# A long convolution and an MLP on one NeuronCore: the MLP in two passes through DRAM, its second layer with seven products for eight

## The chip, the cores and the metric

The kernel runs on one core of one Trainium2 chip. The metric is the device time of one execution in microseconds. Engines: TensorE (PE; its weight loads are PEld), VectorE (DVE), ScalarE (ACT), GpSimd (POOL) and SyncE (SP), which here issues almost all DMAs.

## The reference, cut to what matters

The first half (a layer norm, a short and a long causal convolution with gates) makes `x` of 2048 tokens and 640 columns. The second half, which the change touches, is a layer norm and an MLP with 1728 features:

```python
def _B_ref(x, w1, b1, w2, b2):
    h = jnp.einsum("bsd,df->bsf", x, w1) + b1
    zero = jnp.zeros_like(h)
    r = jnp.where(h > zero, h, zero)
    h = r * r
    out = jnp.einsum("bsf,fd->bsd", h, w2) + b2
    return out
...
h = _layernorm(x, axis=-1) * (1 + cb) + sb
x = x + gb * _B_ref(h, B_w1, B_b1, B_w2, B_b2)
```

## The kernel before, in words

Everything is float32. The first half works on five blocks of 128 columns; its order is written out in a table (`at`, with places `FS(b, j)` and `GS(b, s)`). It leaves the residual `x1` partly in SBUF and partly in the DRAM tile `x1_d`. The table's last places also load and split the first MLP weights.

The MLP multiplies in three terms: a number is split into a part in the type fp32r (`hi`, a copy by ACT) and the rest (`lo = x − hi`, a subtraction by DVE or POOL), and hi·hi, hi·lo and lo·hi are added up in PSUM. So each weight tile, each transposed input `XT` and each activation `h` costs one ACT copy and one subtraction.

The MLP runs over 8 chunks of 256 tokens (`NC`, `CH`) and, in each, over 14 groups of 128 features (`NF`; the last has 64). For one (chunk, group):

- `mlp_front` (L721): 5 blocks of input columns × 3 terms = 15 matmuls, stationary a 128x128 piece of w1, moving 256 tokens; the last group needs 10 (L712), the first two go through L735.
- `mlp_front_end` (L753, and L749 and L751 for the last group): ACT adds the bias and takes the positive part, out of PSUM; POOL squares it (`mul`, L150).
- `mlp_split` (L145, L156): ACT copy and DVE subtraction of 128x256.
- `mlp_back` (L791): three groups later (`MLAG`), stationary `h` of 128 features × 128 tokens, moving 320 columns of w2: 2 token halves × 2 column halves × 3 terms = 12 matmuls into four PSUM accumulators; the last group needs 8.

At a chunk's end `mlp_gate` (L806) multiplies the accumulators by the gate row, `mlp_out` adds the residual and stores. Beside the groups of one chunk run the statistics, the normalisation (`prep_hat`, L673), the transposes (`prep_xt1`, L686, L688) and the splits of the next one. The order is that of the loop at the end; `keep_order` fixes it on each engine, so an instruction that waits holds up all behind it on its engine. The helpers `copy` (L145), `mul` (L150), `add` (L153), `sub` (L156) and `sp_dma` (L138) record most operations. In the changed kernel the same helpers stand three lines lower.

Of the kernel before, what the change touches and what calls it, by code (L numbers as in the profile page):

```python
# [18 lines left out]
P = 128  # L19
# [4 lines left out]
NF = 14  # L24
# [3 lines left out]
MLAG = 3  # L28
# [64 lines left out]
def ssm_mlp_kernel(  # L93
# [38 lines left out]
    x1_d = dr.tile([S, D], F32, tag="x1_d", name="x1_d")  # L132

# [388 lines left out]

    ys, tss = {}, {}
# [62 lines left out]
    WI = {}  # L586
    slots = []

    def w_tile(tag, n):
        t = sb.tile([P, n * 1280], F32R, tag=tag, name=f"w_{tag}")  # L590
        for i in range(n):
            slots.append(t[:, 1280 * i : 1280 * (i + 1)])

    wn = [0, 0]
    stage = []

    def w_load(kind, f):
        m = P if f < NF - 1 else 64
        s = sb.tile([P, D], F32, tag="STG", name=f"w{kind}s_{f}", bufs=4)
        dst = slots.pop(0)  # L600
        if kind == 1:
            sp_dma(
                s[:, 0 : 5 * m].rearrange("p (k f) -> p k f", k=NB),
                w1[:, f * P : f * P + m].rearrange("(k p) f -> p k f", p=P),
            )
            s = s[:, 0 : 5 * m]
            d = dst[:, 0 : 10 * m].rearrange("p (h x) -> p h x", h=2)
            WI[1, f] = dst[:, 0 : 10 * m].rearrange("p (h k f) -> p h k f", h=2, k=NB)
            if m < P:
                s = s.rearrange("p (k f) -> p k f", k=NB)  # L610
                d = dst[:, 0 : 10 * m].rearrange("p (k h f) -> p h k f", h=2, k=NB)
                WI[1, f] = dst[:, 0 : 10 * m].rearrange("p (k x) -> p k x", k=NB)
        else:
            for j in range(P // m):
                sp_dma(s[j * m : (j + 1) * m], w2[f * P : f * P + m, :])
            d = WI[2, f] = dst.rearrange("p (h x) -> p h x", h=2)
        stage.append((kind, m, s, d))

    def w_high():
        kind, m, s, d = stage[wn[0]]  # L620
        wn[0] += 1
        copy(act, d[:, 0], s)

    def w_low(eng):
        kind, m, s, d = stage[wn[1]]
        stage[wn[1]] = None
        wn[1] += 1
        sub(eng, d[:, 1], s, d[:, 0])
        if kind == 2 and m == 64:
            dve.tensor_scalar(d[64:128, 1], s[64:128], 0.0, None, op0=ALU.mult)  # L630

    items = [(kind, f) for f in range(NF) for kind in (1, 2)]

    def load_item():
        if items:
            w_load(*items.pop(0))
# [25 lines left out]
    def load_x1(n):  # L662
        if n >= 2:
            X1t[n] = x1_tile(n)
            sp_dma(
                X1t[n], x1_d[n * CH : (n + 1) * CH, :].rearrange("(l p) d -> p l d", p=P)
            )

# [8 lines left out]
    def prep_xt(n, b):  # L677
        prep_xt1(n, b)
        prep_xt2(n, b)

    def prep_xt1(n, b):
        if b == 0:
            XT[n] = sb.tile([P, 2, NB, CH], F32R, tag=f"XP{(n + 1) % 2}", name=f"xt_{n}")
        t = ps.tile([P, 2, P], F32, tag="Y", name=f"xtp_{n}_{b}", bufs=2)
        for i in range(2):
            pe.transpose(t[:, i], ML["xh"][i][:, b * P : (b + 1) * P], ident)  # L686
        f = ML["xf"][b % 2]
        dve.tensor_scalar(  # L688
            f,
# [7 lines left out]
    def prep_xt2(n, b):  # L697
        f = ML["xf"][b % 2]
        copy(act, XT[n][:, 0, b], f)
        sub(pool, XT[n][:, 1, b], f, XT[n][:, 0, b])  # L700
# [3 lines left out]
    accs, hs, rs, hps = {}, {}, {}, {}  # L704

    def mlp_front(n, f, b):
        m = P if f < NF - 1 else 64
        if b == 0:
            hps[n, f] = ps.tile([P, CH], F32, tag="T", name=f"h_{n}_{f}", bufs=2)
# [63 lines left out]
    def mlp_back(n, f):  # L773
# [11 lines left out]
        if f == NF - 1:  # L785
            order.sort(key=lambda o: (o[0], o[2]))
# [481 lines left out]
```

## Time and profile before

| | |
|---|---|
| time, three runs | 701.93, 707.03, 709.17 us, median 707.03 |
| the profiled execution, its span from first to last instruction | 711.1 us |
| mean granted TensorE clock | 0.996 |
| instructions | 21018, of them 9164 matmuls |
| busy: PE, DVE, ACT, POOL | 660.6, 332.2, 330.2, 310.1 us |
| the part before the MLP's first matmul | 299 us |
| DMA | 74.75 MB, 105 GB/s in the mean |

Durations below come from the profiled execution. A row of a group gives line, engine, operation, the tiles it writes and reads with their shapes, the count, and its durations. The chain of waits is followed back from the last instruction; the releaser behind an idle time is what ended it.

### The profile page before, as it was taken

Reading aid. Unit: us, or ns where it says so; the run is one execution under the profiler, and the core shown is the slowest. Engines: PE = TensorE matmul, PEld = TensorE weight load, DVE = VectorE, ACT = ScalarE, POOL = GpSimd, SP = SyncE. Lnnn points to the kernel's source line nnn. Section 1 sums busy time; section 2 is a strip of 40 time slices with the busy share of each in tenths; the row PEclk is TensorE's granted clock in tenths of the full one; section 3 lists DMA queues with packets and bytes.
Section 4 is the critical chain, followed back from the end, with each engine's and each line's share of the span. In section 5 each row is a group of like instructions: output and inputs, shape, how many; then the busy total and the mean of one; then the engine's idle time right before and its main releaser. Section 6 shows DMA issues by size and latency. Waiting matters only on the chain.

```text
span 711.1 us, 21018 instructions
## 1 busy us (share of the span) xinstructions
PE 660.6 (93%) x9164; PEld 632.6 (89%) x9164; DVE 332.2 (47%) x601; ACT 330.2 (46%) x688; POOL 310.1 (44%) x390
## 2 busy tenths in 40 slices
PE   6698798998999988999999999999999999999997
PEld 5587697887889888889999999999999999999996
DVE  4275665657576677577532322322323332322313
ACT  4535556877876976357323333333233233233221
POOL 1071155469669858553522513414415315225213
PEclk9999999999999999999999999999999999999999
DMA  9797897689554644366020010010100200200101
GB/s 251 200 274 243 237 266 205 193 236 233 158 150 106 163 132 143 109 179 190 1 75 1 14 61 1 38 38 1 60 15 1 75 1 2 75 1 1 38 1 38
DMA packets 88720, 74.75 MB, mean 105 GB/s; under 512 B 19250, under 2 KB 73906, under 8 KB 88628
## 3 DMA queue, kind: packets, MB, share of 16 engines
q1 hardware_dynamic: 86672, 72.86, 35.7%
q8 instruction: 72, 1.18, 0.7%
q10 hardware_dynamic: 1892, 0.54, 0.3%
q14 instruction: 20, 0.16, 0.1%
q0 software_dynamic: 64, 0.01, 0.0%
HBM read 58.98 MB, written 14.42 MB: 103 GB/s over the span
## 4 chain that ended last, share of the span: by engine, by line
PE 86%; DVE 4%; ACT 4%; issue 3%; DMA 2%; POOL 0%; DVEq 0%; ACTq 0%; POOLq 0%; SPq 0%
PE acc L791 26%; PE h L721 25%; PE y L542 6%; PE pa L386 6%; PE x L401 5%; PE qp L467 5%; PE h L401 4%; PE t L531 3%; PE h L712 1%; PE xtp L686 1%; PE kt L242 1%; PE vt L279 1%; DVE wx L150 1%; DVE kacc L264 1%; PE gr L929 1%
## 5 line engine op out<-in xcount | busy, mean ns | idle before, releaser
L150 POOL TENSOR_TENSOR mtmp<-mtmp 128x256 f32<-128x256 f32 x112 | 71.5, 638 | 244.4 <-ACT mtmp L753 236.2
L721 PE MATMUL h<-xt,w_S 128*128 128x256 f32 x1290 | 167.6, 282 | 1.1 <-DVE w_S L156 1.1
L721 PEld LDWEIGHTS h<-xt,w_S 128*128 128x128 f32 x1290 | 161.7, 190 | 1.3 <-DVE w_S L156 1.3
L791 PE MATMUL acc<-w_S,hring 128*128 128x320 f32 x960 | 156.7, 311 | 0.2 <-DVE hring L156 0.2
L791 PEld LDWEIGHTS acc<-w_S,hring 128*128 128x128 f32 x960 | 142.1, 189 | 0.7 <-DVE hring L156 0.7
L156 DVE TENSOR_TENSOR hring<-mtmp,hring 128x256 fp32r<-128x256 f32 x112 | 66.4, 592 | 162.7 <-ACT hring L145 162.7
L753 ACT ACTIVATE mtmp<-h,b1t 128x256 f32<-128x256 f32 x104 | 49.3, 474 | 179.4 <-PE h L721 176.3
L145 ACT ACTIVATE hring<-mtmp 128x256 fp32r<-128x256 f32 x112 | 46.5, 416 | 48.8 <-POOL mtmp L150 47.8
L386 PE MATMUL pa<-wx,p 64*64 64x64 f32 x2560 | 51.0, 226 | 18.9 <-issue 11.8
L386 PEld LDWEIGHTS pa<-wx,p 64*64 64x64 f32 x2560 | 44.4, 138 | 26.1 <-issue 19.9
L145 ACT ACTIVATE a<-pa 128x512 f32<-128x512 f32 x80 | 43.3, 602 | 31.2 <-PE pa L386 30.7
L542 PE MATMUL y<-wx,wx 128*64 128x64 f32 x1280 | 45.2, 225 | 5.7 <-issue 4.4
L150 DVE TENSOR_TENSOR wx<-x,wx 128x512 f32<-128x512 f32 x64 | 41.0, 684 | 19.2 <-ACT wx L145 8.8
L542 PEld LDWEIGHTS y<-wx,wx 128*64 128x64 f32 x1280 | 40.4, 138 | 10.7 <-issue 6.7
L688 DVE TENSOR_SCALAR we<-xtp,cbs 128x256 f32<-128x256 f32 x35 | 19.0, 543 | 61.1 <-PE xtp L686 61.1
L401 PE MATMUL x<-a,gb 128*64 128x128 f32 x640 | 41.8, 274 | 2.9 <-DVE wx L150 1.8
L401 PEld LDWEIGHTS x<-a,gb 128*64 128x64 f32 x640 | 36.1, 137 | 4.1 <-PE h L401 2.4
L264 DVE SCALAR_TENSOR_TENSOR KV<-kt,tap,KV 128x511 f32<-128x511 f32 (+2 forms) x48 | 35.9, 748 | 8.0 <-ACT ktail L145 6.3
L145 ACT ACTIVATE q<-qp 128x512 f32<-128x512 f32 (+1 forms) x40 | 21.3, 584 | 33.4 <-PE qp L467 33.4
L156 POOL TENSOR_TENSOR we<-wx 128x256 f32<-128x256 f32 x20 | 15.8, 789 | 47.5 <-DVE wx L150 45.7
L153 POOL TENSOR_TENSOR wm<-wm,wm 128x640 f32<-128x640 f32 x20 | 32.6, 1631 | 8.7 <-ACT wm L344 8.4
L401 PE MATMUL h<-a,gb 128*64 128x128 f32 x512 | 34.9, 280 | 0.1
(142 smaller groups left out, 1026.3 us busy)
## 6 DMA issues: line engine op xcount, KB each, us to landing
wm<-in_w_mod_dram SPq DMA_DIRECT2D x25, 320.0 KB, 5.3
KV<-in_A_k_dram SPq DMA_DIRECT2D x20, 256.0 KB, 5.4
KV<-in_A_v_dram SPq DMA_DIRECT2D x20, 256.0 KB, 4.9
xp<-in_A_q_dram SPq DMA_DIRECT2D x5, 1024.0 KB, 7.5
out_dram<-x SPq DMA_DIRECT2D x14, 320.0 KB, 2.5
w1s<-in_B_w_dram SPq DMA_DIRECT2D x13, 320.0 KB, 3.7
w2s<-in_B_w_dram SPq DMA_DIRECT2D x13, 320.0 KB, 3.9
kv_d<-KV SPq DMA_DIRECT2D x16, 256.0 KB, 5.4
```

Source lines behind the costliest of these rows:

```text
L145: act.activation(o, i, AF.Copy)
L150: eng.tensor_mul(o, a, b)
L153: eng.tensor_add(o, a, b)
L156: eng.tensor_sub(o, a, b)
L264: dve.scalar_tensor_tensor(o, tk[:, : 512 - t], tap[:, b, t : t + 1], o, op0=ALU.mult, op1=ALU.add)
L386: pe.matmul(t[e][64 * r : 64 * r + 64, g].rearrange("p m d -> p (m d)"), pt[b][l, i, 8 * q + g, :], cw[l, r], start=True, stop=True,)
L401: pe.matmul(t[64 * a : 64 * a + 64, s + r], gb[:, g, r, a], AX[b][i][:, 2 * g + a], start=True, stop=True,)
L467: pe.matmul(t[a][:, u], gi[l, 4 * j + u, r], w[r][l, u % 2], start=(r == 0), stop=(r == 1),)
L542: pe.matmul(y[64 * h : 64 * h + 64, 4 * (g % 2) + i].rearrange("p c l d -> p (c l d)"), tss[g][:, i, 64 * r : 64 * r + 64], ca[:, r, h], s ...
L721: pe.matmul(hps[n, f][:m], WI[1, f][:, a, b], XT[n][:, x, b], start=(b == 0 and i == 0), stop=(b == NB - 1 and i == 2),)
L753: act.activation(r[:m], h[:m], AF.Relu, bias=b1t[:m, f : f + 1])
L791: pe.matmul(acc[2 * s + i], h[:, a, s * P : (s + 1) * P], w[:, y, i * 320 : (i + 1) * 320], start=(f == 0 and ti == 0), stop=(f == NF - 1 ...
```

## The change

**First pass.** Before anything of the second layer runs, the first layer is done for all tokens. A list `steps` gives its order: the first five feature groups for tokens 0 to 255 and 256 to 511 (ten steps of 256 tokens), the same groups for the other three tiles of 512 tokens (15 steps), then groups 5 to 8 and 9 to 13 for all four tiles (36 steps). A matmul moves 512 tokens from step 10 on. `mlp_front_end` squares on DVE up to step 24 and on POOL from then on, and stores the plain square to a DRAM tile `h_d`. The split of `h` is gone from this pass. All of `XT` stays in SBUF; w1 of the groups 9 to 12 goes into the slots of 0, 1, 2 and 5. The residual with `b2` times the gate is added per chunk (`resid`, one POOL operation of 1280 columns) and stored to `x1_d` again. Six chunks' residuals are fetched at the end of the first half.

**Second pass.** It goes over 8 chunks of 256 tokens and, in each, over six pairs of feature groups and one plain step for groups 12 and 13. A pair and two token halves and two column halves are a 2x2 block product, done with seven products of sums instead of eight. `w2_sums` forms the four sums on the w2 side once, in the first pass. `c_sums` forms four sums of 128x128 on the `h` side for each chunk and pair, on POOL, in a tile of seven such pieces; `c_split` makes hi and lo of all seven (128x896); `products` issues 7 × 3 matmuls into seven of eight PSUM accumulators, the plain step 20 into the last four. `evict_first` and `evict_rest` put the accumulators together. All eight PSUM banks are accumulators of one chunk. The loop runs ahead: `c_split` two steps, `c_sums` three, `c_load` four.

```diff
-MLAG = 3
+TW = 512
+NT = S // TW
+NP = 6
...
+    def c_sums(n, k):
+        if k == NP:
+            return
+        c = CT[n, k].rearrange("p (j s) -> p j s", j=7)
+        sub(pool, c[:, 4], c[:, 0], c[:, 1])
+        add(pool, c[:, 1], c[:, 1], c[:, 3])
+        sub(pool, c[:, 5], c[:, 1], c[:, 0])
+        sub(pool, c[:, 6], c[:, 2], c[:, 5])
+
+    def c_split(n, k):
+        c = CT.pop((n, k))
+        hi, lo = HT[n, k] = ML["h"][(7 * n + k) % 4]
+        if k < NP:
+            copy(act, hi, c)
+            sub(dve, lo, c, hi)
+            return
...
+        if k < NP:
+            for j, place in enumerate(PLACE):
+                c = slice(place * P, (place + 1) * P)
+                w = W2[k, j]
+                for i, (a, y) in enumerate(((0, 0), (0, 1), (1, 0))):
                     pe.matmul(
-                        acc[2 * s + i],
-                        h[:, a, s * P : (s + 1) * P],
-                        w[:, y, i * 320 : (i + 1) * 320],
-                        start=(f == 0 and ti == 0),
-                        stop=(f == NF - 1 and ti == len(terms) - 1),
+                        acc[j],
+                        h[a][:, c],
+                        w[:, y],
+                        start=(k == 0 and i == 0),
+                        stop=(k == NP - 1 and i == 2 and j < 4),
                     )
...
+    def evict_first(n):
+        acc = accs[n]
+        t1, t5, u2, u3, u4, v = (ML["e"][i] for i in range(6))
+        E[n] = t1, u3, u4, v
+        copy(act, t1, acc[0])
+        add(dve, u2, acc[1], t1)
+        copy(act, t5, acc[3])
+        add(dve, u3, acc[2], u2)
+        add(pool, u4, u2, t5)
+        add(pool, v, u3, t5)
...
+                add(dve, o[:, c], acc[4 + 2 * s + i], ((t1, u4), (u3, v))[s][i])
...
+                mul(dve, o, o, row0b)
+                add(pool, t[:, s], t[:, s], o)
+                sp_dma(out[(2 * n + s) * P : (2 * n + s + 1) * P, :], t[:, s])
...
+    def resid(n):
+        add(pool, X1t[n], X1t[n], row1b[0].unsqueeze(1).to_broadcast([P, 2, D]))
...
+    for m, (n, k) in enumerate(seq):
+        if m + 2 < len(seq):
+            c_split(*seq[m + 2])
+        if m + 3 < len(seq):
+            c_sums(*seq[m + 3])
+        if m + 4 < len(seq):
+            c_load(*seq[m + 4])
+        if k == 0:
+            x2_load(n)
+        products(n, k)
+        if k == NP - 1:
+            evict_first(n)
+        if k == NP:
+            evict_rest(n)
```

The order on POOL around the end of a chunk, before (`mtmp` is the ring of squares, `x1` the residual of a chunk, `gb2row` the gated bias row, `xt` the split input):

```order
L153 TENSOR_TENSOR x1_3_6008<-x1_3_6008,gb2row_4581 128x640
L150 TENSOR_TENSOR mtmp_4760<-mtmp_4760 64x256
L150 TENSOR_TENSOR mtmp_4760<-mtmp_4760 128x256 x2
L153 TENSOR_TENSOR x1_3_6008<-mtmp_4760,x1_3_6008 128x640
L150 TENSOR_TENSOR mtmp_4760<-mtmp_4760 128x256 x7
L156 TENSOR_TENSOR xt_5_7185<-we_69,xt_5_7185 128x256
```

and in the second pass of the change (`c_UP0` and `c_UP1` hold the pieces of two steps each, `e` the evicted accumulators, `wx1` the gated block, `wx2` the residual):

```order
L159 TENSOR_TENSOR c_UP1_5744<-c_UP1_5744 128x128
L156 TENSOR_TENSOR c_UP1_5744<-c_UP1_5744 128x128
L159 TENSOR_TENSOR c_UP1_5744<-c_UP1_5744 128x128 x2
L159 TENSOR_TENSOR c_UP0_5743<-c_UP0_5743 128x128
L156 TENSOR_TENSOR c_UP0_5743<-c_UP0_5743 128x128
L159 TENSOR_TENSOR c_UP0_5743<-c_UP0_5743 128x128 x2
L156 TENSOR_TENSOR e_2_6502<-e_1_6501,e_0_6500 128x320 x2
L159 TENSOR_TENSOR c_UP0_5743<-c_UP0_5743 128x128
L156 TENSOR_TENSOR c_UP0_5743<-c_UP0_5743 128x128
L159 TENSOR_TENSOR c_UP0_5743<-c_UP0_5743 128x128 x2
L156 TENSOR_TENSOR wx2_68<-wx2_68,wx1_67 128x640 x2
L159 TENSOR_TENSOR c_UP1_5744<-c_UP1_5744 128x128
```

One square per step has become four sums per step, and the eviction's four operations stand between the sums of the next chunk's steps 1, 2 and 3.

The order of SP's DMAs around the end of a chunk, before:

```order
L138 DMA out_0_dram<-x1_2_5507 128x640 x2
L138 DMA x1_4_6509<-x1_d_64 128x2x640
L138 DMA out_0_dram<-x1_3_6008 128x640 x2
L138 DMA x1_5_7010<-x1_d_64 128x2x640
L138 DMA out_0_dram<-x1_4_6509 128x640 x2
```

and in the second pass of the change:

```order
L141 DMA c_UP1_5744<-h_d_65 128x2x256
L141 DMA out_0_dram<-wx2_68 128x640 x2
L141 DMA c_UP1_5744<-h_d_65 128x2x256
L141 DMA wx3_69<-x1_d_64 128x2x640
L141 DMA c_UP0_5743<-h_d_65 128x2x256
L141 DMA c_UP0_5743<-h_d_65 128x256
L141 DMA c_UP0_5743<-h_d_65 64x256
```

Behind the two output stores now stands a load of `h` that the next chunk's step 4 needs; before, it was the next chunk's residual.

The order on POOL where the MLP starts, in the change (`xt` with a tag are the splits of the chunks 1, 2 and 3, `x1_2` and `x1_5` hold three chunks' residuals each, `xp_4` and `up_4` the first half's last block):

```order
L153 TENSOR_TENSOR gb2row_4575<-gb2row_4575,gbrow_4811 128x640
L156 TENSOR_TENSOR x1_0_2934<-x1_0_2934,gb2row_4575 128x1280
L156 TENSOR_TENSOR x1_1_2938<-x1_1_2938,gb2row_4575 128x1280
L159 TENSOR_TENSOR xt_S3_4536<-we_70,xt_S2_4510 128x256 x5
L156 TENSOR_TENSOR x1_2_4648<-x1_2_4648,gb2row_4575 128x1280
L159 TENSOR_TENSOR xt_KV_4927<-we_70,xt_KV_4927 128x256 x5
L156 TENSOR_TENSOR x1_2_4648<-xp_4_4037,up_4_4306 128x2x128
L159 TENSOR_TENSOR xt_KV_4927<-we_70,xt_KV_4927 128x256
L156 TENSOR_TENSOR x1_2_4648<-x1_2_4648,gb2row_4575 128x1280
L159 TENSOR_TENSOR xt_KV_4927<-we_70,xt_KV_4927 128x256 x4
```

Residual adds of 1280 columns now stand between the splits of the first chunks; before, POOL's squares of the first chunk and the last three adds of the first half stood here.

More of the change, by code (lines that the diff above doesn't have):

```diff
@@ L1144, in ssm_mlp_kernel @@
         )
-    for i in range(3):
-        w_tile(f"WX{i}", 1)
-    XT[0] = sb.tile([P, 2, NB, CH], F32R, tag="XP1", name="xt_0")
+    w_tile("WX0", 5)
     gate_sum(0, 3)
@@ L1151, in ssm_mlp_kernel @@
     tp += [tl[:, 0], tl[:, 1]]
[L1152 removed]
+    xf = ML["xf"] + [mt[:, 1280:1536]]
     def xt_f(b):
```

541 lines of the change are left out of this document (322 added, 219 removed).

## The prediction

> **What bounds the kernel now.** I read the page's first rows, then the stretches of the second half, then its chain and waits. In the stretch rows each engine has busy time and a count in brackets; then come TensorE's granted clock, the DMA share and GB/s.
>
> ```profile
> span 711.1 us, 21018 instructions
> PE 660.6 (93%) x9164; PEld 632.6 (89%) x9164; DVE 332.2 (47%) x601; ACT 330.2 (46%) x688; POOL 310.1 (44%) x390
> ...
> 298.95 3.99 PE L735 MATMUL h<-xt,w_S 128*128 128x256 f32 x30
> ...
> 303.00:317.50 14.50, 13.20 (x98) 12.50 (x96) 12.43 (x20) 9.16 (x19) 8.77 (x8) 1.00 0.59 169
> 450.30:501.40 51.10, 49.78 (x381) 49.55 (x381) 15.75 (x33) 16.61 (x37) 17.48 (x23) 1.00 0.07 27
> 705.20:711.10 5.90, 0.80 (x6) 0.53 (x4) 2.79 (x6) 0.00 (x0) 1.92 (x2) 0.85 0.30 111
> ```
>
> The MLP begins with its first matmul at 299.0 and lasts to 711.1: 412.1 us, the part that the change rebuilds. A chunk of 256 tokens takes 51.1 us, with PE busy for 49.8 at full clock, and POOL for only 17.5. PE is the bound.
>
> ```profile
> 317.51 1.76 PE acc L791 x12
> 319.27 1.76 PE h L721 x15
> 321.04 1.76 PE acc L791 x12
> ...
> 430.45 1.77 PE acc L791 x12
> 432.22 1.79 PE h L721 x15
> 434.23 1.76 PE acc L791 x12
> PE xtp L686 <- ACT mtmp L673: 7.9, 6, 1.3
> ```
>
> These are links of the chain (start, length). 15 matmuls of 256 columns take 321.04 − 319.27 = 1.77 us, 117.7 ns each; 12 of 320 columns take 1.76 us, 146.9 ns each. The difference is 0.456 ns a column, so the fixed part is 117.7 − 256 × 0.456 = 1 ns: time goes by columns, not by matmuls. Two transposes put in cost 434.23 − 432.22 − 1.79 = 0.22 us.
>
> The 412.1 us are thus: first layer 8 chunks × (13 × 15 + 10) = 1640 matmuls, 193.0; second layer 8 × (13 × 12 + 8) = 1312, 192.7; 35 pairs of transposes, 7.7; tail 5.9; and 12.8 in which PE stands still, 7.9 of it before transposes.
>
> **The change part by part.** *First layer.* A matmul takes 512 columns where it took 256, so 1640 become 150 of 256 and 745 of 512. By the slope a wide one costs 2 × 117.7 = 235.4 ns and nothing is gained. Bounds: no fixed part at all, or one of at most 31 ns, the period of the smallest matmuls of this trace (64 in 2.0 us):
>
> ```profile
> 8.79 2.00 PE pa L386 x64
> ```
>
> That would be worth 745 × 31 ns = 23 us. I take zero, by the two rows whose matmuls are of the same kind. The Trainium skill ("TensorE: Matmul & The Clock Gate", section on the back-to-back issue gap) gives columns/2.4 + 2.5 ns, so 215.8 for 512; by it pass one would be 745 × 19.6 ns = 14.6 us shorter, but it also gives 135.8 for 320 columns where this trace has 146.9.
>
> *Second layer.* Per chunk, 6 pairs of feature groups × 7 products × 3 terms = 126 matmuls, and 20 for the last two groups: 146 for 164. Over 8 chunks 1168 × 146.9 ns = 171.6 us, 21.1 less. This is the whole gain that PE can show; it is PE work on the path, so it counts in full if operands arrive. A chunk's PE time becomes 21.45 us.
>
> *What feeds it.* Each of the 48 steps (21 matmuls, 3.08 us of PE) now needs four POOL sums of 128x128, a ScalarE copy of 128x896 and a VectorE subtraction of 128x896. ScalarE first:
>
> ```profile
> L145 ACT ACTIVATE hring<-mtmp x112: 399/418/421, 304.1 to 703.4; 128x256 fp32r<-128x256 f32 x104, 64x256 fp32r<-64x256 f32 x8
> L145 ACT ACTIVATE w_S<-w1s x11: 720/730/740, 248.5 to 328.5; 128x640 fp32r<-128x640 f32 x11
> ```
>
> 0.42 at 256 and 0.73 at 640 give 0.94 at 896, hidden under 3.08 of PE. POOL (min/median/max in ns):
>
> ```profile
> L153 POOL TENSOR_TENSOR p<-p,dsm x8: 208/235/721, 8.5 to 220.9; 128x8 f32<-128x8 f32 x4, 128x32 f32<-128x32 f32 x4
> L156 POOL TENSOR_TENSOR xt<-we,xt x35: 733/739/1187, 330.3 to 651.0; 128x256 fp32r<-128x256 f32 x35
> L153 POOL TENSOR_TENSOR wm<-wm,wm x20: 1534/1550/2002, 101.7 to 242.4; 128x640 f32<-128x640 f32 x20
> L153 POOL TENSOR_TENSOR x<-mtmp,x x9: 857/1572/1582, 354.8 to 706.6; 128x640 f32<-128x640 f32 x7, 128x320 f32<-128x320 f32 x2
> 39.67 0.73 POOL L156 TENSOR_TENSOR we<-wx 128x256 f32<-128x256 f32 x1
> 40.36 0.72 POOL L153 TENSOR_TENSOR we<-wx 128x256 f32<-128x256 f32 x1
> 148.22 3.17 POOL L153 TENSOR_TENSOR wm<-wm,wm 128x640 f32<-128x640 f32 x2 [4.91 <-ACT wm L344]
> ```
>
> 8, 256, 320 and 640 columns take 0.21, 0.73, 0.86 and 1.55: 0.2 plus 2.1 ns a column, so 0.46 at 128. The trace has no 128; the bounds are 0.36 (half of 256) and 0.73 (256 itself), and the line through four rows decides for 0.46. Independent neighbours start 0.69 apart for 0.73 of work; two that depend take 3.17 for 2 × 1.55, 0.05 extra. Three of the four sums wait for the one before: 0.46 + 3 × 0.51 = 1.99 us a step. A chunk's eviction adds two 320-wide sums and two 640-wide adds: 2 × 0.86 + 2 × 1.55 = 4.8. POOL alone: 6 × 1.99 + 4.8 = 16.8 us, below 21.45.
>
> But VectorE and POOL collide:
>
> ```profile
> 304.05 1.29 POOL L153 TENSOR_TENSOR xp<-xp,up 128x512 f32<-128x512 f32 x1
> 304.57 1.05 DVE L156 TENSOR_TENSOR hring<-mtmp,hring 128x256 fp32r<-128x256 f32 x1 [4.49 <-ACT hring L145]
> 305.29 0.80 POOL L150 TENSOR_TENSOR mtmp<-mtmp 128x256 f32<-128x256 f32 x1
> 305.56 1.21 DVE L156 TENSOR_TENSOR w_S<-w1s,w_S 128x640 fp32r<-128x640 f32 x1
> 306.06 1.87 POOL L153 TENSOR_TENSOR xp<-xp,up 128x512 f32<-128x512 f32 x1
> L156 DVE TENSOR_TENSOR hring<-mtmp,hring x112: 412/426/1679, 304.6 to 703.9; 128x256 fp32r<-128x256 f32 x104, 64x256 fp32r<-64x256 f32 x8
> L150 POOL TENSOR_TENSOR mtmp<-mtmp x112: 606/613/1191, 303.5 to 702.8; 128x256 f32<-128x256 f32 x104, 64x256 f32<-64x256 f32 x8
> L806 DVE TENSOR_TENSOR mtmp<-acc,gbrow x32: 477/482/492, 353.8 to 706.9; 128x320 f32<-128x320 f32 x32
> ```
>
> The subtraction that takes 0.43 alone ends at 305.62, 0.28 after the POOL add that ends at 305.34; POOL's next ends at 306.09, 0.47 after it; the 640-wide at 306.77, 0.68 after that. They take turns, whole instruction by whole instruction. The multiply that reads one operand from PSUM never slows (477 to 492). The Trainium skill ("SBUF — State Buffer", the section on SBUF's two sides) has this rule: the port pair that the two engines share is an exclusive lock held for the whole instruction, by a VectorE operation with two SBUF inputs as well. The rows agree; without that lock the chunk's POOL time would stay 16.8.
>
> Held time is 0.28 at 256 and 0.68 at 640, so 0.95 at 896; POOL's next sum then starts prepared (0.47 for the square that alone takes 0.61, 0.13 back), and the 0.05 of dependence is hidden: 0.77 a step. With the two 640-wide multiplies by the gate (0.68 − 0.13 each) and two 256-wide subtractions (0.15 each), 6 × 0.77 + 1.4 = 6.0 a chunk. POOL with its waits: 22.8 us against PE's 21.45. So POOL falls behind by up to 1.4 us a chunk.
>
> *At a chunk's end* POOL stands in order behind two adds that need the finished block; queued behind them are the sums for step 3 of the next chunk. SyncE stands behind the output stores, and queued there is the load for step 4:
>
> ```profile
> x_d<-xp SPq DMA_DIRECT2D x15, 256.0 KB, 3.4
> KV<-in_A_k_dram SPq DMA_DIRECT2D x20, 256.0 KB, 5.4
> ```
>
> From the block's last matmul: a VectorE sum (0.48) and two 640-wide multiplies (0.43 + 0.40 each) 2.1, POOL adds 3.1, issue 0.4, load 3.4, sums 2.0, copy and subtraction 0.94 + 1.09, together 13.0 us, against four steps of PE, 12.3: 0.7 late, 2.7 with the slower load. With the 1.4 that POOL falls behind I take 2.0 a boundary, 14 for seven, between 0 (POOL's backlog absorbed in its lead of three steps, loads in time) and 19 (the slow load each time).
>
> *Start and entry.* In the first 15 steps POOL must do the row product (1.6), six residual adds of 1280 columns (2.9 each), 25 splits (0.70), three adds (0.73), and give way to VectorE for ten 256-wide squares (0.15), five 512-wide (0.42) and two weight splits (0.55): 43.4 us, from here on:
>
> ```profile
> 299.93 1.58 POOL L150 TENSOR_TENSOR gb2row<-gb2row,gbrow 128x640 f32<-128x640 f32 x1 [7.87 <-ACT gbrow L145]
> 305.00:320.00 15.00, 13.70 (x101) 13.06 (x100) 12.99 (x22) 9.29 (x19) 7.86 (x8) 1.00 0.73 212
> ```
>
>  PE needs the last split at 299.0 + 3.5 + 8 × 1.77 + 5 × 3.53 + 25 × 0.22 + 2.8 = 342.6. POOL is through at 343.3 if it never waits, and it will wait for the copies ahead of its splits: 1 to 8 us of stall, I take 4. Traffic there is 3 MB of fetched residual, stores and weights, near the 212 GB/s that the second row has, which could cost a few us of the 8.
>
> In the rest of pass one a step's work is hidden under 3.53 of PE: POOL's square of 512 (1.2), at times two weight sums of 320 (0.86 each) beside it. h is 1728 × 2048 × 4 bytes = 14.2 MB, out and back some 70 GB/s over 400 us, where the steady row above has 27 and the start's 212: hidden too, except for the load at the boundary. On entering pass two POOL has the squares of the last two steps among its first sums: those for step 2 end some 6 us in, copy and subtraction make it 8, and PE is there at 6.2: about 2. The tail gets one more 320-wide addition, 0.5.
>
> *Sum.* 193.0 + 7.7 + 171.6 + 6.4 + 4 + 14 + 2 = 398.7, for 412.1: 13.4 less. The profiled span, 711.1, lies 4.1 above the median shown, 707.0; I take the same saving off that: 693.6, rounded to 693.5.
>
> **Rivals.** (1) *POOL keeps up*: PE never waits at boundaries, and start and entry cost 6 together. 384.7, a saving of 27.4: 679.6 us. For it: POOL alone needs 16.8 of 21.45. Against it: the alternation above.
> (2) *Wide matmuls are cheaper*: a fixed part near 20 ns, 15 us beyond the forecast: 678.5. Against it: the two-row slope.
> (3) *What TensorE saves is given back*: sums of 0.55 instead of 0.46 put POOL at 24 × 0.09 = 2.2 more, 25.0 us a chunk, 3.5 beyond PE: 25 for seven where I have 14, and a start of 6 for 4: 693.5 + 11 + 2 = 706.5, no change. For it: 0.55 lies inside the bounds. Against it: the line.
> (4) *POOL sets the pace, slower*: if a 128-wide sum costs nearly what a 256-wide one does, a step is 0.73 + 3 × 0.78 + 0.77 = 3.84 and a chunk 23.0 + 6.2 = 29.2, 7.8 beyond PE; seven are 55 where I have 14: 734. It decides from 0.58 a sum on: (0.58 − 0.46) × 24 = 2.9 more a chunk, 20 in seven, which against the saving of 13.4 puts the time 7 above now. For it: VectorE is one more claimant in that queue, and every sum waits on semaphores. Against it: the four rows on one line.
>
> **How the numbers follow.** The forecast gets 0.47 with its own range 684 to 703, rival 1 0.15, rival 2 0.05, rival 3 0.15, rival 4 0.18. A measurement here tells about 1% from no change, so faster means under 700 and slower above 714. Most of the forecast, with rivals 1 and 2, is faster: 0.60. Rival 3 and the forecast's edge: 0.21. Slower: 0.19. Below 678 lies a tenth; above 722 another, rival 4's upper half: the range is 678 to 722.
>
> **What would show it.** In the changed profile: 512-column matmuls 235 ns apart (216 would be rival 2); 128-wide POOL sums of 0.46 alone and chains of four near 2.0, stretched to 2.8 when the 896-wide subtraction falls among them; that subtraction at 1.1 alone and up to 1.5 when it waits; chunks of pass two 23 to 24 us long with PE busy for 21.5; PE's waits in pass two on VectorE's and ScalarE's split, steps 3 and 4 of a chunk first; POOL busy for over 85% there. A pass two with chunks of 21.5 means rival 1, of 25 or more rivals 3 or 4. A stall at one place above 8 us, or pass one over 215 us (I have 205), would make the prediction wrong.

## The result and the profile after

| | before | after |
|---|---|---|
| median of 4 runs, us | 706.7 (701.9 to 709.2) | 747.2 (745.1 to 752.3) |
| ratio | | 1.057, 95% interval 1.051 to 1.063 |
| profiled execution: span, time | 711.1 | 744.6, 746.3 |
| first matmul of the MLP | 298.95 | 296.07 |
| from there to the first product of pass two | | 235.0 |
| from the first product to the end of the span | | 213.5 |

The change makes the kernel 5.7% slower, 40.5 us by the medians. I had forecast 693.5 us, and a range up to 722.

The first rows of the page after the change, to be read beside those of before:

```profile
span 744.6 us, 19800 instructions
PE 658.9 (88%) x8275; PEld 588.3 (79%) x8275; DVE 408.9 (55%) x634; ACT 335.0 (45%) x631; POOL 440.9 (59%) x545
```

TensorE has 889 matmuls fewer in the records, most of those of the first layer twice as wide, and is busy for about as long (658.9 for 660.6). POOL went from 310 to 441 us, VectorE from 332 to 409.

The stretches of the MLP on one table (busy time and count for each engine, granted TensorE clock, DMA share, GB/s):

```profile
303.00:315.00 12.00, 6.32 (x48) 5.59 (x47) 8.92 (x17) 3.99 (x11) 5.84 (x6) 0.97 0.40 151
315.00:328.00 13.00, 10.41 (x53) 10.12 (x54) 9.98 (x18) 5.39 (x12) 6.68 (x7) 0.64 0.14 50
328.00:340.00 12.00, 7.92 (x46) 7.04 (x45) 6.89 (x16) 6.04 (x12) 8.74 (x9) 0.86 0.16 57
340.00:355.00 15.00, 11.89 (x52) 9.28 (x51) 7.20 (x16) 6.60 (x13) 8.25 (x7) 0.89 0.42 138
367.00:384.00 17.00, 12.06 (x51) 9.16 (x50) 11.23 (x19) 8.52 (x15) 7.96 (x7) 0.90 0.39 119
400.00:522.00 122.00, 122.00 (x538) 100.58 (x537) 35.95 (x50) 43.67 (x83) 57.85 (x57) 1.00 0.38 120
582.50:608.40 25.90, 23.80 (x148) 22.87 (x148) 14.07 (x17) 6.98 (x10) 20.49 (x29) 0.93 0.38 120
738.30:744.60 6.30, 0.01 (x1) 0.00 (x0) 3.30 (x7) 0.00 (x0) 0.86 (x1) 0.70 0.30 105
```

Three things stand here. From 400 to 522 us pass one runs without a stall, as forecast: TensorE is busy for 122.00 of 122.00, at full clock. Before that, in the steps in which the transposes of the later chunks are made, it stands still for a fifth to a half of a stretch and its clock sinks, at the lowest to 0.64. And a chunk of pass two lasts 25.9 us for the 21.45 of matmuls that I had counted. Its clock of 0.93 is not the reason: three of the chunks have 0.93 or 0.94 and last 25.9 to 26.4 us, three have 1.00 and last 25.8 to 26.0.

What TensorE waits for from 296 to 389 us (us, times, longest), and the links of the chain in that time (start, length):

```profile
PE xtp L725 <- DVE we L726: 19.5, 7, 4.9
PE h L775 <- ACT xt_S L148: 2.9, 1, 2.9
PE xtp L725 <- ACT mtmp L718: 1.4, 3, 0.5
```

```profile
303.85 2.88 DVE wx L153
...
317.01 2.82 DVE wx L153
...
369.05 2.99 DVE wx L153
...
388.86 133.31 PE h L775 x585
```

The long stall is at the transposes, which wait until VectorE has emptied their two PSUM tiles (L726). VectorE comes late because of squares (`wx`, L153) that last 2.8 to 3.0 us. The timeline of one such place shows why:

```profile
303.53 2.92 POOL L156 TENSOR_TENSOR x<-x,gb2row 128x1280 f32<-128x1280 f32 x1 [1.86 <-ACT mtmp L718]
303.85 2.88 DVE L153 TENSOR_TENSOR wx<-wx 128x256 f32<-128x256 f32 x1 [1.49 <-ACT wx L806]
306.65 0.41 DVE L156 TENSOR_TENSOR x<-xp,up 128x256 f32<-128x256 f32 x1
306.99 1.61 DVE L726 TENSOR_SCALAR we<-xtp,cbs 128x256 f32<-128x256 f32 x3
307.58 0.44 PE L725 MATMUL xtp<-ident,mtmp 128*128 128x128 f32 x2 [2.10 <-DVE we L726]
```

POOL adds the bias row to a chunk's residual in one operation of 1280 columns, 303.53 to 306.45. A square of 256 columns that VectorE starts at 303.85 ends at 306.73, just after POOL has done. The evictions stand behind it in VectorE's order, the transposes behind those in TensorE's order, and with them every matmul. At the longest wait, 4.9 us until 375.31, the square holds VectorE from 369.05 to 372.04, and 2.7 us of a later chunk's statistics still stand between it and the evictions.

At a chunk's end, the links of the chain (after the last matmul) and SyncE's queue with what POOL does meanwhile (the first view leaves out links under about a microsecond):

```profile
582.88 1.67 DVE wx L156 x4
584.55 1.04 DVE wx L153
586.47 1.23 issue
587.71 2.42 POOL wx L156
590.59 3.71 DMA c_UP<-h_d
597.97 1.20 POOL c_UP L156
601.25 1.10 DVE h_XP L159
602.40 3.06 PE acc L864 x19
```

```profile
585.66 4.46 POOL L156 TENSOR_TENSOR wx<-wx,wx 128x640 f32<-128x640 f32 x2 [0.76 <-DVE wx L153]
586.24 2.46 DVE L159 TENSOR_TENSOR h_x<-c_UP,h_x 128x896 fp32r<-128x896 f32 x1
587.77 2.72 SPq L141 DMA_DIRECT2D out_dram<-wx  x2
590.59 0.65 SPq L141 DMA_DIRECT2D c_UP<-h_d  x1
```

The forecast had this chain; but POOL's two additions take 4.46 us, not 3.1, while an 896-wide subtraction of VectorE falls among them and lasts 2.46 for 1.09: the two take turns.

### The profile page after: what moved, and what is told of

Its sections match the earlier page's. It is cut to its first block, busy times and chain, and to the rows that moved or that the text cites. A ratio compares the mean times of both kernels' runs of the same rounds, so it can differ in the third digit from the quotient of the medians.

```text
span 744.6 us, 19800 instructions
## 1 busy us (share of the span) xinstructions
PE 658.9 (88%) x8275; PEld 588.3 (79%) x8275; DVE 408.9 (55%) x634; ACT 335.0 (45%) x631; POOL 440.9 (59%) x545
## 4 chain that ended last, share of the span: by engine, by line
PE 54%; DVE 13%; DMA 10%; ACT 7%; POOL 7%; issue 6%; SPq 1%; DVEq 0%; POOLq 0%; ACTq 0%
PE h L775 21%; PE pa L389 5%; DMA c_UP<-h_d 5%; PE acc L864 5%; PE qp L470 4%; DVE wx L153 4%; PE y L566 4%; PE x L404 4%; POOL wx L156 3%; PE acc L877 3%; PE h L404 3%; POOL c_UP L159 2%; PE t L555 2%; DVE wx L156 2%; DVE s L302 2%
## 5 line engine op out<-in xcount | busy, mean ns | idle before, releaser
L159 POOL TENSOR_TENSOR c_UP<-c_UP 128x128 f32<-128x128 f32 x144 | 91.3, 638 | 36.2 <-DMA c_UP<-h_d 26.6
L153 POOL TENSOR_TENSOR wx<-wx 128x512 f32<-128x512 f32 (+1 forms) x36 | 40.5, 1124 | 73.5 <-ACT wx L806 68.4
L775 PE MATMUL h<-xt_S,w_S 128*128 128x512 f32 (+1 forms) x285 | 77.7, 378 | 3.1 <-ACT xt_S L148 2.9
L806 ACT ACTIVATE wx<-h,b1t 128x512 f32<-128x512 f32 (+1 forms) x57 | 36.8, 647 | 85.0 <-PE h L775 78.0
L864 PE MATMUL acc<-w_S,h_S 128*128 128x320 f32 x360 | 60.2, 318 | 9.6 <-ACT h_S L148 5.7
L389 PE MATMUL pa<-wx,p 64*64 64x64 f32 x2560 | 52.7, 233 | 14.1 <-issue 8.3
L864 PEld LDWEIGHTS acc<-w_S,h_S 128*128 128x128 f32 x360 | 54.7, 192 | 13.3 <-ACT h_S L148 7.0
L159 DVE TENSOR_TENSOR h_S<-c_UP,h_S 128x896 fp32r<-128x896 f32 (+2 forms) x32 | 37.3, 1170 | 49.6 <-ACT h_S L148 49.5
L775 PEld LDWEIGHTS h<-xt_S,w_S 128*128 128x128 f32 x285 | 51.4, 211 | 10.0 <-ACT xt_S L148 3.1
L148 ACT ACTIVATE a<-pa 128x512 f32<-128x512 f32 x80 | 43.3, 601 | 29.5 <-PE pa L389 29.4
L153 DVE TENSOR_TENSOR wx<-x,wx 128x512 f32<-128x512 f32 x64 | 41.0, 684 | 16.9 <-ACT wx L148 6.5
L566 PEld LDWEIGHTS y<-wx,wx 128*64 128x64 f32 x1280 | 40.4, 138 | 10.7 <-issue 6.5
L153 DVE TENSOR_TENSOR wx<-wx 128x512 f32<-128x512 f32 (+1 forms) x25 | 28.6, 1149 | 34.5 <-ACT wx L806 34.5
L775 PE MATMUL h<-xt_XP,w_S 128*128 128x512 f32 x120 | 41.2, 394 | 0.0
L864 PE MATMUL acc<-w_S,h_x 128*128 128x320 f32 x180 | 31.8, 327 | 9.0 <-ACT h_x L148 5.9
```

The lines of the kernel that those rows point to most:

```text
L148: act.activation(o, i, AF.Copy)
L153: eng.tensor_mul(o, a, b)
L159: eng.tensor_sub(o, a, b)
L389: pe.matmul(t[e][64 * r : 64 * r + 64, g].rearrange("p m d -> p (m d)"), pt[b][l, i, 8 * q + g, :], cw[l, r], start=True, stop=True,)
L566: pe.matmul(y[64 * h : 64 * h + 64, 4 * (g % 2) + i].rearrange("p c l d -> p (c l d)"), tss[g][:, i, 64 * r : 64 * r + 64], ca[:, r, h], s ...
L775: pe.matmul(hps[key], w, y, start=(b == 0 and i == 0), stop=(b == NB - 1 and i == len(terms) - 1),)
```

## The experiments

Each row below is one profiled execution (the last kernel's time is a median of 6). "First stretch" goes from the MLP's first matmul to the first product of pass two, "chunk" is the mean of seven chunks of pass two, "rest" goes from the first product to the end of the span. The first column shows how far the work before the MLP, which none of the edits touches, moves from execution to execution: 291.1 to 301.2 us. That is why causes are read from the stretches and not from the whole; the forecast for the whole was missed more than once (s3, b1, w1) where that for the stretch or the chunk was met or nearly met. Kernels that share a part show how far it moves by itself: the unchanged first stretch 235.0 to 236.4 (after, b1, b2, b4), the repaired one 209.3 and 210.0 (d1, d2), the unchanged rest 212.5 to 215.2 (after, s1, s2, s3, d1), the repaired one 184.1 to 184.3 (b4, d2, w1).

| kernel | MLP begins | first stretch | chunk | rest | time |
|---|---|---|---|---|---|
| after | 296.1 | 235.0 | 25.8 | 213.5 | 746.3 |
| s1 no residual addition | 298.7 | 220.9 | 26.0 | 215.2 | 736.7 |
| s2 residual in pieces | 291.3 | 226.1 | 25.6 | 212.5 | 731.5 |
| s3 squares by ScalarE | 291.1 | 217.3 | 25.8 | 213.2 | 723.4 |
| b1 late stores | 293.7 | 236.2 | 23.7 | 198.8 | 730.5 |
| b2 additions by VectorE | 301.2 | 235.9 | 24.4 | 203.4 | 742.7 |
| b4 both of these | 294.7 | 236.4 | 21.6 | 184.3 | 717.6 |
| d1 start repaired | 296.7 | 209.3 | 25.8 | 213.5 | 721.3 |
| d2 all repairs | 293.0 | 210.0 | 21.6 | 184.1 | 688.9 |
| w1 d2, 256-wide matmuls | 300.1 | 216.7 | 21.6 | 184.3 | 702.9 |
| f1 d2, last squares moved | 294.5 | 208.1 | 21.6 | 182.6 | 687.0 |

The chunk's mean comes from the first and the last of the 16 copies by which ScalarE empties two accumulators a chunk. The last is the second copy of its chunk and comes nine matmuls of 146.9 ns, 1.3 us, after the first one. In the kernel after the change, (734.1 − 552.2 − 1.3) / 7 = 25.8:

```profile
L148 ACT ACTIVATE e<-acc x16: 417/428/438, 552.2 to 734.1; 128x320 f32<-128x320 f32 x16
```

### The start: who holds the port

The theory: POOL's addition of 1280 columns holds the port that the two engines share, and VectorE, working in order, carries the wait on to the transposes. The rivals: latency of the chain or traffic (A), the amount of POOL's work whatever its pieces (B), VectorE's statistics and ScalarE's rows (C).

**s1.** The addition is left out, so the output lacks that term.

```diff
     def resid(n):
-        add(pool, X1t[n], X1t[n], row1b[0].unsqueeze(1).to_broadcast([P, 2, D]))
+        return
```

> Left out: the addition of the gated bias row to the residual (eight POOL additions of 128x1280, 2.95 us each, between 296 and 389 us), so the output lacks that term. Theory (these additions hold the port that POOL and VectorE share; VectorE's squares and statistics stand behind them, its evictions of the transposes stand behind those, and TensorE waits): the stall of 33 us in the first 93 us of the MLP shrinks by 20 or more, pass one lasts 205 to 212 us instead of 232, the whole 718 to 727 us. Rival A (the stall is the delay of a chain of small hand-overs, or traffic of the residual): at most 6 us less, pass one 226 or more, the whole above 738. Pass two: chunks of 26 us as before by either.

The first stretch fell by 14.1 us, to 220.9: more than rival A allows, less than I had expected. VectorE's groups from 296 to 389 us, first in the kernel after the change, then (298 to 392) in this one:

```profile
L153 DVE TENSOR_TENSOR wx<-wx 128x512 f32<-128x512 f32 x8 | 12.0, 1499 | 11.4 <-ACT wx L806 11.4
L153 DVE TENSOR_TENSOR wx<-wx 128x256 f32<-128x256 f32 x10 | 11.7, 1181 | 7.3 <-ACT wx L806 7.3
```

```profile
L153 DVE TENSOR_TENSOR wx<-wx 128x512 f32<-128x512 f32 x12 | 8.6, 716 | 18.3 <-ACT wx L806 18.3
L153 DVE TENSOR_TENSOR wx<-wx 128x256 f32<-128x256 f32 x10 | 6.9, 696 | 7.9 <-ACT wx L806 7.9
```

The mean square of 256 columns goes from 1181 ns to 696, that of 512 from 1499 to 716 (twelve of them in this stretch, where there were eight). So the additions are a cause, but not the only one; 696 is still well above the 420 or so that a two-operand VectorE operation of 256 columns takes undisturbed. POOL's splits of 0.73 us, which remain, would explain that; no run leaves them out.

**s2.** The same addition in four pieces of 320 columns: more POOL work, shorter holds.

```diff
-        add(pool, X1t[n], X1t[n], row1b[0].unsqueeze(1).to_broadcast([P, 2, D]))
+        for l in range(2):
+            for c in (slice(0, 320), slice(320, 640)):
+                add(pool, X1t[n][:, l, c], X1t[n][:, l, c], row1b[0][:, c])
```

> The same addition as four of 128x320 (0.86 us each by the rows before, 3.45 a chunk instead of 2.95; POOL has 4 us more to do in the start). Theory that the length of one hold matters (VectorE gets its turn after 0.86 us): squares of 256 take at most 1.3 us where they take up to 2.9, pass one 210 to 225 us, the whole 725 to 740. Rival B (what matters is how much POOL does, not in what pieces): pass one 232 to 238, the whole 746 to 752.

226.1 us, 8.9 less, although POOL spends 30.9 us on the additions where it spent 23.6. Here, POOL's two rows, after the change and in this kernel:

```profile
L156 POOL TENSOR_TENSOR x<-x,gb2row 128x1280 f32<-128x1280 f32 x8 | 23.6, 2947 | 11.1 <-DMA x_d<-x 4.7 <-issue 3.0 <-ACT mtmp L718 2.9
```

```profile
L156 POOL TENSOR_TENSOR x<-x,gb2row 128x320 f32<-128x320 f32 x32 | 30.9, 995 | 5.4 <-ACT mtmp L718 5.4
```

A piece takes 995 ns for the 860 that 320 columns take alone: it waits for VectorE now and then. Rival B falls: what cost the time was the length of a hold, not the sum of POOL's work. The stretch just missed my upper bound of 225.

**s3.** The first 25 steps are squared by ScalarE. Its squares here never take more than 634 ns, so they don't wait for POOL.

```diff
-        mul(eng, r[:m], r[:m], r[:m])
+        if eng is act:
+            act.activation(r[:m], r[:m], AF.Square)
+        else:
+            mul(eng, r[:m], r[:m], r[:m])
...
-            mlp_front_end(*a, pool if i - 1 >= 25 else dve)
+            mlp_front_end(*a, pool if i - 1 >= 25 else act)
```

> The squares of the first 25 steps by ScalarE (about 0.42 us at 256 columns, 0.6 at 512: 9 us more for ScalarE over 93) instead of VectorE, which then has far fewer operations with two SBUF operands there. Theory (VectorE's order behind squares that wait for the port): TensorE's waits for the evictions of the transposes, 19.5 us in 7, fall below 8; pass one 212 to 222 us, the whole 726 to 737. Rival C (VectorE's statistics and small operations wait for the port all the same, or ScalarE becomes late with the normalised rows): pass one above 226.

217.3 us, 17.7 less, and TensorE's wait for the evictions, from 291 to 384 us, is

```profile
PE xtp L725 <- DVE we L726: 7.9, 4, 3.4
```

where it was 19.5. This is the strongest single edit: it takes away most of the waiting side. Rival C is right in a remainder: an operation on two columns still waits for POOL's 1280, as VectorE's group in the same stretch shows:

```profile
L710 DVE SCALAR_TENSOR_TENSOR nm<-mv,rs 128x2 f32<-128x2 f32 x7 | 6.6, 946 | 0.2
```

946 ns on average for what takes 160 ns when POOL is idle.

### A chunk's end: the queue behind the store, or POOL's pace

**b1.** The stores of a finished block are issued behind step 2 of the next chunk, so that the loads of `h` go first.

```diff
                 add(pool, t[:, s], t[:, s], o)
-                sp_dma(out[(2 * n + s) * P : (2 * n + s + 1) * P, :], t[:, s])
...
         if k == NP:
             evict_rest(n)
+        if k == 2 and n:
+            for s in range(2):
+                sp_dma(out[(2 * n - 2 + s) * P : (2 * n - 1 + s) * P, :], X2[n - 1][:, s])
```

> In pass two the stores of a finished block are issued two to three steps later, behind the loads of h that stood queued after them. Theory (the store waits for POOL's last addition, and the load behind it on SyncE's queue comes too late): POOL's waits for loads in pass two fall from 22.7 us to under 8, chunks of 26.05 become 24 to 25, the whole 735 to 742. Rival D (POOL with the port is the pace, 24 sums and four additions against VectorE's holds): chunks stay above 25.7, since POOL only waits for something else; the whole above 744.

POOL's waits for loads in pass two, after the change and in this kernel:

```profile
POOL c_UP L159 <- DMA c_UP<-h_d: 22.7, 13, 2.4
```

```profile
POOL c_UP L159 <- DMA c_UP<-h_d: 1.2, 2, 0.9
```

The chunk went from 25.8 to 23.7, a little more than expected, and 2.25 us are left over TensorE's 21.45. Where, the stretches of two chunks of this kernel tell (POOL is the last engine ahead of the clock):

```profile
575.50:599.30 23.80, 21.93 (x148) 21.40 (x147) 13.79 (x16) 7.03 (x12) 21.63 (x29) 1.00 0.41 132
599.30:623.00 23.70, 21.90 (x148) 21.37 (x147) 13.76 (x16) 6.95 (x11) 21.53 (x29) 1.00 0.40 130
```

POOL has hardly a load to wait for any more, and is busy, port waits included, for 21.6 of 23.7 us. That is not yet the pace of rival D: at each boundary POOL still stands idle for VectorE before its two additions (the last two of the nine waits are the tail's):

```profile
POOL wx L156 <- DVE wx L153: 6.7, 9, 0.9
```

What TensorE waits for in this kernel is the same at each of the seven boundaries: step 3 of the new chunk, 1.2 to 1.4 us for ScalarE's copy and then 0.6 for VectorE's subtraction. The sums of step 3 stand on POOL behind the two additions, which need the finished block and take 4.46 us here too. So the second cause beside the late loads is these additions, their length and their place in POOL's order, and not that POOL has too much to do in sum.

**b2.** The two 640-wide additions of the residual by VectorE, stores where they were.

```diff
                 mul(dve, o, o, row0b)
-                add(pool, t[:, s], t[:, s], o)
+                add(dve, t[:, s], t[:, s], o)
                 sp_dma(out[(2 * n + s) * P : (2 * n + s + 1) * P, :], t[:, s])
```

> In pass two the two 640-wide additions of the residual by VectorE instead of POOL; the stores stay where they were. Each holds the port for about 0.7 us instead of the 2.25 that POOL takes, and the stores leave earlier. Theory (late stores delay the loads behind them, and POOL with the port is the pace): both parts shrink, chunks of 26.05 become 22 to 23.5, the whole 718 to 732. Rival F (VectorE is the engine that is late at a block's end, and two more additions make it later): chunks of 25.5 or more, the whole above 740.

Between both forecasts: 24.4 us a chunk. POOL is freed, but the stall moves to the loads:

```profile
POOL c_UP L159 <- DMA c_UP<-h_d: 38.3, 15, 4.0
```

38.3 us of waiting where it was 22.7. The load behind the stores is issued at 593.63, 6.7 us after the products of the next chunk begin (586.89); in the kernel after the change that was 590.59 for 582.33, 8.3. The 1.5 between them is about the gain, 1.4 us a chunk; the load still stands behind the stores, and POOL, with less to do, waits for it.

**b4.** Both edits together.

> Late stores (alone they gave chunks of 23.9 us with POOL busy, port waits included, for 21.8 of 24.0) and the two residual additions by VectorE, together. Theory (what is left after the late stores is POOL's pace, whose two additions of 2.25 us go and two holds of 0.7 come: 3.1 less): chunks of 21.5 to 22.2 us, TensorE's own 21.45, the whole 714 to 724. Rival G (what is left is the chain sums, ScalarE copy, VectorE subtraction at a chunk's beginning, whoever adds): chunks stay at 23.3 or more, the whole above 726.

Stretches of two of its chunks:

```profile
618.00:639.40 21.40, 21.40 (x148) 21.40 (x147) 15.17 (x18) 7.14 (x11) 19.63 (x27) 1.00 0.46 147
639.40:660.80 21.40, 21.40 (x148) 21.40 (x148) 15.10 (x19) 7.23 (x11) 19.79 (x27) 1.00 0.46 146
```

21.4 us, TensorE busy in every one of them; the mean of the seven is 21.6. Rival G (the chain of sums, copy and subtraction by itself) falls: with the same chain, but without the additions on POOL, TensorE now never waits in these chunks.

### Both repaired

**d1.** The start alone: s3, the additions for chunks 2, 3 and 4 in pieces as in s2, the others put off to steps 20 to 24.

```diff
-        do(i, (resid, n))
-        do(i + 1, (x1_store, n))
+        j = {1: 21, 5: 22, 6: 23, 7: 24}.get(n, i)
+        do(j, (resid, n))
+        do(j + 1, (x1_store, n))
...
-    do(2, (resid, 0))
-    do(3, (x1_store, 0))
+    do(20, (resid, 0))
+    do(21, (x1_store, 0))
...
-    do(21, (u_tile2, "S5", 6))
-    do(25, (u_tile2, "S0", 6), (h_tiles,))
+    do(33, (u_tile2, "S5", 6), (u_tile2, "S0", 6), (h_tiles,))
```

> Only the start: squares of the first 25 steps by ScalarE, the residual additions of chunks 0, 1, 5, 6, 7 put off to steps 20 to 24, when POOL has nothing to do, and those of chunks 2, 3, 4 in four pieces of 320. Alone the squares brought the stretch from the first matmul of the MLP to the first product from 235.0 to 217.3 us, no residual 220.9, pieces 226.1; TensorE's own work there is 195. Theory (both ends of the fight for the port cost): together 202 to 210 us, the whole 712 to 724. Rival H (after the squares have gone the additions hold up nobody, and what is left is the chain from statistics to splits): 214 or more. Pass two: chunks of 26.

209.3 us to the first product, inside the theory's range; rival H falls. What TensorE waits for from 296 to 390 us, and the stretch:

```profile
PE xtp L725 <- DVE we L726: 3.7, 3, 2.2
```

```profile
296.00:389.00 93.00, 85.02 (x468) 70.70 (x466) 41.97 (x102) 58.83 (x116) 54.89 (x57) 1.00 0.39 133
```

19.5 us of waits have become 3.7, and the granted clock is 1.00 over the whole stretch. It was 0.89 from 296 to 389 us after the change and 0.94 to 0.96 in the same part of s1, s2 and s3: the low clocks came and went with the stalls. The DMAs move more than in the changed kernel, 133 GB/s for 106, so traffic (rival A) was not the cause. In the table of the changed kernel, length times the missing share of the clock adds up to 12 × 0.03 + 13 × 0.36 + 12 × 0.14 + 15 × 0.11 + 17 × 0.10 = 10.1 us at most that the low clock itself can have cost; how much of it did, no run separates.

**d2.** d1 and b4.

> The start of the run before and in pass two the late stores with VectorE's residual additions. Theory: the savings add, 202 to 210 us to the first product and chunks of 21.5 to 22.2: 680 to 694 in all, below the kernel before the change (705.6 on this chip). Rival I (the stall moves: traffic and entry to pass two give part of it back): above 698.

The two parts add up: 210.0 us and chunks of 21.6. Of the profiled times 746.3 and 688.9, 25.0 of the difference are from the first stretch, 29.4 from the rest, and 3.1 from the earlier start. The kernel before took 706.9 on the same chip (one execution each). Rival I falls.

**w1.** d2 with each wide matmul as two of 256 columns, to settle the price that the prediction argued over.

```diff
         for i, (w, y) in enumerate(terms):
-            pe.matmul(
-                hps[key],
-                w,
-                y,
-                start=(b == 0 and i == 0),
-                stop=(b == NB - 1 and i == len(terms) - 1),
-            )
+            for c in range(0, c1 - c0, CH):
+                pe.matmul(
+                    hps[key][:, c : c + CH],
+                    w,
+                    y[:, c : c + CH],
+                    start=(b == 0 and i == 0 and c == 0),
+                    stop=(b == NB - 1 and i == len(terms) - 1 and c + CH == c1 - c0),
+                )
```

> The repaired kernel (ScalarE squares, put-off residual additions, late stores, VectorE additions; 209.95 us from the first matmul of the MLP to the first product) with each 512-wide matmul of the first layer as two of 256 columns into the halves of the same tile; all else as it was. The row of the changed kernel gives 227.9 ns for a wide one, the row of the kernel before 117.7 for a narrow one: 745 x (235.4 - 227.9) = 5.6 us. Theory (wide ones save 7.5 ns each): 214 to 217 us to the first product, the whole 692 to 697. Rival J, that of the prediction (time goes by columns alone, and the difference is in how the rows were cut): 209 to 211 us, the whole 687 to 691.

The longest link of the chain in d2 and in w1:

```profile
360.50 133.29 PE h L780 x585
```

```profile
368.69 139.57 PE h L781 x1170
```

585 wide ones take 227.8 ns each, the same work as 1170 narrow ones 139.57 / 585 = 238.6 ns a pair, 119.3 each. A wide matmul saves 10.7 ns, over 745 of them 8.0 us; the stretch rose by 6.8. The theory holds and rival J falls. (The whole, 702.9, lies above what I had given, by the MLP's beginning 7 us later.)

**f1.** d2, and the squares of the last four steps of pass one by ScalarE.

```diff
-            mlp_front_end(*a, pool if i - 1 >= 25 else act)
+            mlp_front_end(*a, pool if 25 <= i - 1 < len(steps) - 4 else act)
...
-    mlp_front_end(*steps[-1], pool)
+    mlp_front_end(*steps[-1], act)
```

> The repaired kernel, and the squares of the last four steps of pass one by ScalarE too, so that POOL is free for the first sums of pass two, where TensorE stood 3.4 us before the first product and POOL's chain ran with two squares of 1.2 us in it. Theory: the entry loses 1 to 3 us less, the whole 684 to 690 against 706.5 before, ratio 0.968 to 0.978. Rival K (the first product waits for the load and ScalarE's copy of weights, not for POOL): the entry as it was, 687 to 691.

The first product of pass two in d2 and in f1, from the timeline of TensorE:

```profile
502.95 0.90 PE L872 MATMUL acc<-w_S,h_x 128*128 128x320 f32 x2 [3.40 <-ACT h_x L148]
```

```profile
502.63 0.56 PE L872 MATMUL acc<-w_S,h_x 128*128 128x320 f32 x2 [0.56 <-ACT h_x L148]
```

The wait before it fell from 3.4 us to 0.6, the first stretch by 1.8 and the rest by 1.6, a little more than expected; rival K falls. This version takes 687.0 us, median of 6 runs (680.6 to 689.1), against 708.3 of the kernel before on the same chip: 0.967, interval 0.963 to 0.972. It is the fastest of all, and it keeps the whole change that by itself cost 5.7%.

## Why the prediction was wrong

The forecast was 13.4 us less than a span of 711.1; in the profiled executions it became 33.5 more (40.5 by the medians). The 46.9 between them, term by term (TensorE's own work of pass one is 193.0 + 7.7 less what the wide matmuls save, 745 × 7.5 ns = 5.6, so 195.1):

| term | forecast | measured | difference |
|---|---|---|---|
| stall in the start | 4 | 235.0 − 195.1 − 3.1 = 36.8 | +32.8 |
| wide matmuls | 0 | −5.6 | −5.6 |
| entry to pass two | 2 | 3.1 before the first product, 5.0 behind it | +6.1 |
| seven boundaries | 14 | 7 × (25.8 − 21.45) = 30.5 | +16.5 |
| products and tail | 171.6 + 6.4 | 178.0, taken over | 0 |
| MLP begins | 298.95 | 296.07 | −2.9 |

The 5.0 is what is left of the rest: 213.5 − 178.0 − 30.5. The 36.8 hold more than standing still: from 296 to 389 us TensorE is idle for 24.1 us, 19.5 of them before the transposes, and up to 10.1 are the lowered clock.

**The step that failed first is "Start and entry".** I added up POOL's work there, 43.4 us, set it against the moment at which TensorE needs the last split, and read "1 to 8 us of stall". POOL was not too slow in sum: s2 gave it 7 us more to do and the stretch became 8.9 shorter. The harm goes the other way round. I had quoted rows in which VectorE's subtraction waits for POOL and had used them only to lengthen POOL's time, at 0.15 us a square. What POOL's operations of 2.95 us do to VectorE I didn't price, although the additions of 1280 columns were in my list with their 2.9 us, and neither did I name what stands behind a waiting square on VectorE: statistics, evictions of transposes, and behind those, in TensorE's order, all matmuls. s1, s2, s3 and d1 show that both the holder and the waiter matter: 14.1 us without the one, 17.7 without the other, 25.7 with the waiter gone and most holders put off. Some 11 us of stall and hand-overs are left in d2 (210.0 − 195.1 − 3.4); their cause stays open.

**The boundaries were mis-sized.** Both queues stood in the prediction: on POOL the sums of step 3 behind two additions that need the finished block, on SyncE the load of step 4 behind the stores. I priced only SyncE's, 0.7 us late or 2.7 with a slower load, put POOL's backlog of 1.4 beside it, and took 2.0. It was 4.35. At the boundary shown POOL's additions begin 3.3 us after the new chunk's first product (585.66 for 582.33), where I had 2.1 after the block's last one: VectorE still has a split in hand until 582.96, and then does four sums in 1.67 us where I counted one. The additions take 4.46 us, not 3.1. So the sums of step 3 come late, for which I had no term (TensorE waits 1.4 us for their copy, until 593.17), and the load of step 4 goes out 8.3 us after the first product. It lasts 3.71, near my 3.4. The slow loads of the chain, 5.3 to 6.7 us at the other six boundaries, are those of step 5, issued behind the 640-KB fetch of the next residual; the forecast had nothing for them. The backlog shows neither here nor in b1: POOL waits 0.76 us for VectorE before its additions. That 2.7 and 1.4 come to 4.1, nearly what was measured, is chance. Of the 4.35, late stores took away 2.1 (b1) and moving the additions 2.1 more (b4), and 0.15 is left; the additions moved alone were worth 1.4 (b2).

**The wide matmuls** saved 5.6 us by their row, 6.8 by w1, where I had nothing. The fixed part of 1 ns was finer than its rows: it is 5 × 117.7 − 4 × 146.9, so that 0.01 us in one link of 1.76 moves it by 3.3 ns, and the links shown vary from 1.76 to 1.79.

**The entry** cost 8 us for 2. That POOL has squares among its first sums was in the forecast. f1 shows that it is worth 3.4, and about 4 remain.

**Right were** the prices of the new operations. POOL's sums in pass two (min, median, max in ns):

```profile
L159 POOL TENSOR_TENSOR c_UP<-c_UP x144: 452/462/1398, 528.0 to 729.7; 128x128 f32<-128x128 f32 x144
L156 POOL TENSOR_TENSOR c_UP<-c_UP x48: 452/459/1186, 528.5 to 727.9; 128x128 f32<-128x128 f32 x48
```

0.46 as forecast in the median, copies of 896 in 0.95 and subtractions in 1.09, the tail 6.3. The 171.6 us of products are right too: in b4 a chunk lasts 21.4. So the whole gain on TensorE was there, and all of it was given back.

**The rivals.** None was what happened. Rival 4 ended on the right side, but its condition, a sum of 0.58 us or more, wasn't met, nor was rival 3's of 0.55. So the sign that I gave, "of 25 or more rivals 3 or 4", pointed at the wrong cause: chunks lasted 25.8 with sums of 0.46. Rival 1 is what d2's pass two does after the repair. Rival 2, cheaper wide matmuls, is half true: 7.5 to 10.7 ns each instead of 20. The sentence on what would make the prediction wrong, "pass one over 215 us", applied; "a single stall above 8 us" did not: the longest wait in the start was 4.9.

## What to carry to other kernels

Where two engines take turns at a port, price both directions: not only how much longer the busier engine takes, but how long its longest single operation keeps the other one, and then follow that one's queue, instruction by instruction, to the matmul that stands behind it. A total of busy time against a due date hides this; here four pieces with 30% more work were better than one long operation, and moving the squares to an engine outside the port was better than either. And where two queues stand behind the same late result, here POOL's sums behind its additions and SyncE's loads behind its stores, time both, and repair both: at the chunk's end late stores alone gave 2.1 us, moving the additions alone 1.4, both together 4.2.

## What the runs showed of the hardware that I hadn't expected

- A VectorE operation on 2 columns waits for POOL as long as one on 256. At 299.81 us it took 1.88 us and ended when POOL's 2.95 us addition ended; in steps without POOL it takes 0.16. The lock that the Trainium skill describes ("SBUF — State Buffer", the section on SBUF's two sides), held for a whole instruction, is thus paid by the shortest operation at the length of the longest.
- The granted clock sank to 0.64 over 13 us in a stretch where TensorE kept stopping, and was 1.00 in that part of the kernel once most stops were gone (d1). From 316 to 320 us it was 0.50, with TensorE busy throughout. Fifteen wide matmuls took 4.44 us at 349.79 (chain of the changed kernel), 296 ns each instead of 228, in a stretch whose mean clock was 0.89. The Trainium skill ("TensorE: Matmul & The Clock Gate", Part 1, on the HAM clock gate) has the clock fall to half after an idle window of about 3.4 us. The half rate agrees, and a mean of 0.64 would be half rate for 72% of those 13 us. But no stop of TensorE in the MLP before that place was longer than 2.9 us, so that here shorter stops were enough.
- A matmul of 512 columns takes 227.9 ns and two of 256 take 235 to 239, so that there is a fixed part of 7 to 11 ns in each, where the slope between 256 and 320 columns had left 1 ns. By the formula of the Trainium skill ("TensorE: Matmul & The Clock Gate", section on the back-to-back issue gap) a matmul of 512 columns would take 215.8; the measurement decides.
